# Scores of sparse query blocks: the low part of the queries times the high part of the keys in 64-row tiles, two heads at once, in a new order of all work

## The chip, the cores and the metric

The kernel runs on one core of one Trainium2 chip. The metric is the device time of one execution in microseconds, and three executions were timed: 767.21, 767.59 and 769.55 us, median 767.59 us. One more execution was profiled.

## What is computed

Block-sparse attention over 4 batches of 8 heads, followed by a gated two-layer network (cut; softmax and the last product are written short):

```python
scores = scale * np.matmul(q, k.transpose(0, 1, 3, 2))      # q, k, v: 4 x 8 x 768 x 64
mask = np.abs(blk_i - blk_j) <= window                       # window 1, blocks of 32 rows
mask = mask | (blk_i == 0) | (blk_j == 0) | (blk_i == n_blocks - 1) | (blk_j == n_blocks - 1)
for qb in range(n_blocks):
    for kb in sampled_blocks[qb]:                            # 3 sampled blocks
        mask[qb * block:(qb + 1) * block, kb * block:(kb + 1) * block] = True
scores = np.where(mask, scores, -1000000000.0)
attn = softmax(scores)                                       # over the last axis
x = (attn @ v), heads side by side: 3072 x 512
g = x @ w_gate                                               # 512 x 1536
silu = g * (1.0 / (1.0 + np.exp(-g)))
return (silu * (x @ w_val) @ w_out)                          # 1536 x 512
```

A query block of 32 rows attends to eight key blocks: the first, the last, three around its own and three sampled ones. The first and last query block of each batch attend to everything.

## The kernel before

**Chunks.** The 24 query blocks of a batch are put four to a tile of 128 rows. Batch 0 is worked in three chunks of two tiles (chunks 0 to 2), batches 1 to 3 in two chunks of three tiles each (chunks 3 to 8). For every chunk the kernel does attention and then the network: `ffn_in` (24 products of 12 matmuls each, line 1749; for chunks 0 and 1 in f32, line 1743) and `ffn_out` (per tile of 128 rows 36 matmuls, line 1812).

**Split numbers.** Batch 0 is worked in f32. In batches 1 to 3 every f32 number is held as two f16 numbers, a high and a low part. Keys are split in `load_kv` (ACT line 410 for the high part, DVE line 413 for the low one, two of each per 256 tokens) and turned by a DMA transpose (line 764, issued from SP) so that of each head the 64 partitions 0 to 63 hold the high part and the partitions 64 to 127 the low part. The queries of a tile lie twice, on partitions 0 to 63 and again on 64 to 127, as a high tile and a low tile.

**One sparse query block** (`block`, line 1116). The keys of its eight key blocks are copied to a ring (`keys`, lines 1133 to 1136, DVE), its values come by DMA. `scores` (line 1157) then runs for each half `g` of the heads (even or odd) and each of the two query parts `l` four matmuls, one for every `u`: head `2u+g`, 128 rows by 32 columns at column position `32u`, 256 keys. All 128 partitions are contracted, so that a query part meets both key parts at once. Four such matmuls lie beside each other in the array and run together; a block has 4 such steps of four matmuls. The scores of a block fill one PSUM bank (256 for even heads, 256 for odd heads). DVE adds the mask and takes the maximum (`top`, line 1171), ACT takes the exponential (lines 1186 and 1189) and splits it (410), DVE makes the low part (413), a DMA transposes it (1212), and TensorE multiplies by the values (`product`, line 1224, also 128x32 tiles). Two blocks are a pair: their scores are one task of 32 matmuls, named `qk`, their products share a bank, which DVE sums and scales (1240, 1243) and TensorE transposes (`x_turn`, line 1249). There are 33 pairs in batches 1 to 3.

**Batch 0** (`pair0`) makes its scores with f32 matmuls of 64 rows by 32 columns (line 1388), two heads in the two halves of the rows, each half with its own PSUM bank. `full_rows` and `full_rows0` work the two query blocks that attend to everything.

**The order** of all work is a list written out by hand, `TURN` (2750 tasks). Each engine takes its own tasks in that order and waits at the head of its queue for what the task needs. Buffers are rings: `qk` has two PSUM banks, `pv` two, `ffn` four. The numbers given to `add` as costs are not used by this order.

Of the kernel before, what the change touches and what calls it, by code (L numbers as in the profile page):

```python
# [9 lines left out]
F16 = mybir.dt.float16  # L10
# [242 lines left out]
def tile_block_sparse_attn_swiglu(  # L253
# [865 lines left out]
    def block(ci, b, bt, o, sub, n, qb, col, rank, tsc, pv, both):  # L1119
# [24 lines left out]
        def gathered():  # L1144
            nc.gpsimd.indirect_dma_start(  # L1145
                vf[0:96, 1, :], None, bt.vd, bass.IndirectOffsetOnAxis(ap=vidx[0:96, qb : qb + 1], axis=0)
            )

        qk, e, pp, pts = Buf("qk"), Buf("e"), Buf("pp"), Buf("pts")
        c = {}  # L1150

        def scores():
# [758 lines left out]
```

## Time and profile before

| | |
|---|---|
| median of 3 executions | 767.59 us |
| span of the profiled execution, first to last instruction | 765.5 us |
| what lies around the span, against the median | 2.1 us |
| TensorE (PE) busy | 736.9 us, 96% |
| VectorE (DVE) busy | 567.3 us, 74% |
| ScalarE (ACT) busy | 479.7 us, 63% |
| GpSimd (POOL) busy | 240.0 us, 31% |
| scores of sparse blocks, line 1157: 1056 matmuls | 35.0 us |

An engine is busy while one of its instructions runs. A matmul's record begins when its first column enters the array and lasts until its last result is out, so the records of matmuls that follow each other overlap: what a matmul takes of TensorE is read from the distance of the starts, not from its duration. The chain of waits goes back from the last instruction, at each step to what released it. "Idle before" is time in which the engine stood still just ahead of an instruction, with the instruction that ended the wait.

### The profile page before, as it was taken

The page shows a single profiled execution, that of the slowest core. Times are in us where ns is not written, and L with a number is a line of the kernel's source. Part 1 is how long each engine was busy: PE and PEld are TensorE (multiplying, and loading weights), DVE is VectorE, ACT ScalarE, POOL GpSimd, SP SyncE. Part 2 cuts the span into 40 slices and gives each one's busy share as a digit, 9 for nine tenths or more (in the row PEclk, how much of TensorE's full clock was granted, in tenths as well). Part 3 has the DMA queues.
Part 4 walks back from the last instruction along what each step waited for, and adds up shares of the span by engine and source line. Part 5 has one row for each costly group of instructions (what it writes and reads, how often), then busy time and mean ns, then how long its engine had stood idle before and what let it go on. Part 6 is the DMA issues. An engine that isn't in the chain of part 4 may idle for free.

```text
span 765.5 us, 22137 instructions
## 1 busy us (share of the span) xinstructions
PE 736.9 (96%) x8793; PEld 467.1 (61%) x8793; DVE 567.3 (74%) x1581; ACT 479.7 (63%) x1117; POOL 240.0 (31%) x290
## 2 busy tenths in 40 slices
PE   4899999999999999999999999999999999999998
PEld 3576788774686566545665566545665566555655
DVE  6999999987999998456898878647986677633220
ACT  4999655876887776745796665755764664443211
POOL 4887022222044422211343331302243333202210
PEclk9899999999999999999999999999999999999999
DMA  8856577376499996968779988787766854450001
GB/s 284 252 180 211 186 256 257 102 230 158 95 216 202 199 182 111 208 210 201 172 173 177 226 209 196 137 189 165 157 159 116 192 127 102 82 88 15 1 1 42
DMA packets 156472, 123.75 MB, mean 162 GB/s; under 512 B 113456, under 2 KB 124080, under 8 KB 156368
## 3 DMA queue, kind: packets, MB, share of 16 engines
q1 hardware_dynamic: 150736, 105.03, 57.5%
q0 software_dynamic: 5632, 17.31, 9.3%
q8 instruction: 69, 1.13, 0.6%
q14 instruction: 35, 0.29, 0.1%
HBM read 84.55 MB, written 11.01 MB: 125 GB/s over the span
## 4 chain that ended last, share of the span: by engine, by line
PE 64%; DVE 19%; ACT 5%; DMA 4%; issue 4%; POOL 1%; SPq 1%; DVEq 0%; POOLq 0%; ACTq 0%
PE p L1749 31%; PE po L1812 22%; PE qk L1157 3%; PE pv L1224 2%; DMA ptsf<-ppf 2%; DVE pp L413 1%; DVE act L1758 1%; DVE act L1763 1%; DVE w2all L451 1%; DVE w2all L452 1%; DVE kring L1135 1%; DVE e L1171 1%; PE pv L1249 1%; PE pvf L1011 1%; PE qkf L940 1%
## 5 line engine op out<-in xcount | busy, mean ns | idle before, releaser
L1749 PE MATMUL p<-xall,w1t 128*128 128x384 f16 (+1 forms) x2016 | 323.7, 319 | 1.0 <-DVE act L1758 1.0
L1749 PEld LDWEIGHTS <-w1t 128*128 128x128 f16 x2016 | 193.8, 98 | 117.0 <-issue 5.9
L1771 POOL TENSOR_TENSOR h<-act,h 128x384 f16<-128x384 f32 (+1 forms) x108 | 102.4, 952 | 333.9 <-ACT h L1768 330.4
L1812 PE MATMUL po<-w2all,h 128*128 128x512 f16 (+1 forms) x900 | 192.5, 371 | 0.3 <-DVE act L1758 0.3
L1812 PEld LDWEIGHTS <-h 128*128 128x128 f16 x900 | 86.4, 98 | 93.9 <-issue 1.6
L1145 POOL DMA_INDIRECT w2all<-vd,vidx x66 | 65.0, 985 | 92.6 <-PE pv L1224 83.1
L1743 PE MATMUL p<-xall,w1t 128*128 128x256 f32 x384 | 87.8, 383 | 3.6 <-DVE act L1758 2.5
L1758 DVE SCALAR_TENSOR_TENSOR act<-act,p 128x384 f32<-128x384 f32 (+1 forms) x108 | 54.3, 504 | 47.1 <-ACT act L1754 46.7
L1768 ACT CAST h<-act 128x384 f16<-128x384 f32 (+1 forms) x108 | 50.4, 471 | 61.8 <-DVE act L1763 61.6
L1743 PEld LDWEIGHTS p<-xall,w1t 128*128 128x128 f32 x384 | 71.0, 190 | 15.9 <-DVE act L1758 3.6
L1754 ACT ACTIVATE act<-p,gsc 128x384 f32<-128x384 f32 (+1 forms) x84 | 46.8, 558 | 52.4 <-PE p L1749 31.9
L1189 ACT ACTIVATE e<-e,nb,es 128x256 f32<-128x256 f32 x132 | 78.2, 593 | 2.2
L413 DVE SCALAR_TENSOR_TENSOR pp<-e,pp 128x512 f16<-128x512 f32 x66 | 51.0, 778 | 15.4 <-ACT pp L410 14.2
L1763 DVE SCALAR_TENSOR_TENSOR act<-act,hs,p 128x384 f32<-128x384 f32 (+1 forms) x84 | 49.4, 591 | 11.4 <-PE p L1749 9.1
L1171 DVE CUSTOM_DVE_ANT_1 e<-qk,msk 128x256 f32<-128x256 f32 x132 | 49.3, 418 | 2.5 <-PE qk L1157 2.2
L1687 POOL TENSOR_TENSOR sqx<-sqx 128x768 bf16<-128x768 bf16 (+3 forms) x18 | 22.3, 1238 | 61.0 <-ACT sqx L1683 60.4
L410 ACT ACTIVATE pp<-e 128x512 f16<-128x512 f32 x66 | 40.6, 624 | 0.6
L1135 DVE COPY kring<-kst 128x256 f16 x198 | 38.4, 253 | 3.0 <-PE qk L1157 1.5
L1644 ACT ACTIVATE ot<-po,oc 128x512 f32<-128x512 f32 (+1 forms) x25 | 16.6, 664 | 33.0 <-PE po L1812 27.3
L1519 ACT CAST xall<-pv 128x256 f16<-128x256 f32 x36 | 13.0, 364 | 36.3 <-PE pv L1249 36.3
L1157 PE MATMUL qk<-kring,qs 128*32 128x256 f16 x1056 | 35.0, 273 | 0.0
L1186 ACT ACTIVATE nb<-mx,es 128x2 f32<-128x2 f32 x66 | 19.1, 289 | 25.0 <-DVE mx L1171 24.3
(200 smaller groups left out, 991.5 us busy)
## 6 DMA issues: line engine op xcount, KB each, us to landing
stage<-in_w_dram SPq DMA_DIRECT2D x36, 512.0 KB, 6.6
w2all<-vd SPq DMA_DIRECT2D x66, 192.0 KB, 4.1
qraw<-in_q_dram SPq DMA_DIRECT2D x18, 512.0 KB, 4.5
out_dram<-ot SPq DMA_DIRECT2D x19, 256.0 KB, 2.8
qn<-in_q_dram SPq DMA_DIRECT2D x36, 128.0 KB, 4.1
stage<-in_v_dram SPq DMA_DIRECT2D x9, 512.0 KB, 5.5
vd<-stage SPq DMA_DIRECT2D x9, 512.0 KB, 2.8
stage<-in_k_dram SPq DMA_DIRECT2D x9, 512.0 KB, 6.2
```

The costliest lines, as they stand in the source:

```text
L413: nc.vector.scalar_tensor_tensor(lo, src, scale, hi, op0=ALU.mult, op1=ALU.subtract)
L1145: nc.gpsimd.indirect_dma_start(vf[0:96, 1, :], None, bt.vd, bass.IndirectOffsetOnAxis(ap=vidx[0:96, qb : qb + 1], axis=0))
L1157: nc.tensor.matmul(stv[u * BLK : (u + 1) * BLK, g].rearrange("p s k -> p (s k)"), o.q[:, l, u, g, col : col + BLK], kg[:, 2 * u + g].rearr ...
L1171: nc.vector.tensor_tensor_reduce(ev[:, g], stv[:, g], o.g.msk[:, qb, :].unsqueeze(2).broadcast_to([P, 8, BLK]), scale=1.0, scalar=-3.0e38, ...
L1189: nc.scalar.activation(ev[:, g], ev[:, g], AF.Exp, bias=nb_[:, g : g + 1], scale=o.g.es[:, 0:1], accum_out=both["rs"][:, n % 2, g : g + 1],)
L1743: nc.tensor.matmul(t[:, 0:tc_], w[:, i + 1, k_ * P : (k_ + 1) * P], x_k(k_), start=k_ == 0, stop=k_ == NKT - 1)
L1749: nc.tensor.matmul(t[:, 0:tc_], w_[:, f, m, k_, :], x_k(k_, l), start=i == 0, stop=i == 11)
L1758: nc.vector.scalar_tensor_tensor(a_, a_, 1.0, pg.tile[:, 0:tc_], op0=ALU.add, op1=ALU.mult)
L1763: nc.vector.scalar_tensor_tensor(a_, a_, sc, pw.tile[:, 0:tc_], op0=ALU.mult, op1=ALU.mult)
L1768: nc.scalar.copy(hv(f)[:, 0, :], act.tile[:, 0:tc_])
L1771: nc.gpsimd.tensor_tensor(hv(f)[:, 1, :], act.tile[:, 0:tc_], hv(f)[:, 0, :], op=ALU.subtract)
L1812: nc.tensor.matmul(po.tile[:, cs], hv(f)[:, l, ts_], w2h[:, f, m, cs], start=f == 0 and i == 0, stop=f == NF - 1 and i == 2)
```

## The change

In batches 1 to 3 the high query part is multiplied with all 128 partitions as before (8 matmuls of 128x32 a block, two steps of four). The low query part is multiplied with the high key part alone, 64 partitions, in tiles of 64 rows by 32 columns: an even head in rows 0 to 63, an odd head in rows 64 to 127, so that eight matmuls lie in the array beside each other. The product of the low query part and the low key part falls away. For this the keys of odd heads are stored with the halves swapped (high part on partitions 64 to 127). The two halves of the heads write to two different PSUM banks; the two blocks of a pair share these two banks, each taking 256 columns of each. In `load_kv` a high or low instruction for keys now takes the even or the odd heads of both 128-token halves, and the two DMA transposes of 256 tokens are issued after both low parts. The number of instructions is unchanged everywhere. `TURN` is a new list of the same 2750 tasks; on TensorE 312 of 573 tasks stand at another place, none further than 11 places. The diff without the list:

```diff
@@ -729,10 +729,12 @@
 
         def views(i, tt):
 
-            dst = parts[i].tile.bitcast(F16)
-            pat = "p (t h l d) -> p t h l d" if what == "k" else "p (t l h d) -> p t h l d"
-            dst = dst.rearrange(pat, h=H, l=2, d=D)
-            return dst[:, tt, :, 0, :], dst[:, tt, :, 1, :], raws[i][1]().rearrange("p t (h d) -> p t h d", d=D)[:, tt]
+            dst, src = parts[i].tile.bitcast(F16), raws[i][1]()
+            if what == "k":
+                four = dst.rearrange("p (u g x d) -> p u g x d", g=2, x=2, d=D)[:, :, tt]
+                return four[:, :, tt, :], four[:, :, 1 - tt, :], src.rearrange("p t (u g d) -> p (t u) g d", g=2, d=D)[:, :, tt]
+            dst = dst.rearrange("p (t l h d) -> p t h l d", h=H, l=2, d=D)
+            return dst[:, tt, :, 0, :], dst[:, tt, :, 1, :], src.rearrange("p t (h d) -> p t h d", d=D)[:, tt]
 
         done = []
         for i in range(3):
@@ -755,7 +757,8 @@
                 h_ = add("ACT", 0.63, high, [t] + los, rank, take=pi if first else [], use=ru + ([] if first else pi))
                 l_ = add("DVE", 0.68, low, [h_], rank, use=ru + pi)
                 los.append(l_)
-                if what == "k":
+            if what == "k":
+                for tt in range(2):
 
                     def turn(i=i, tt=tt):
                         if i == 0 and tt == 0:
@@ -767,7 +770,7 @@
                         )
 
                     f0 = i == 0 and tt == 0
-                    done.append(add("SP", 1.3, turn, [l_], rank, behind=None if f0 else done[0], take=[bt.ks] if f0 else [],
+                    done.append(add("SP", 1.3, turn, los, rank, behind=None if f0 else done[0], take=[bt.ks] if f0 else [],
                                     use=pi + ([] if f0 else [bt.ks]), dma=1.7))
             if what == "v":
 
@@ -1105,13 +1108,12 @@
                 if not b:
                     pair0(ci, o, sub, n, sparse[n], qbs.index(sparse[n]) * BLK, r)
                     continue
-                pv, both = Buf("pv"), {}
+                pv, both = Buf("pv"), {"qk": [Buf("qk"), Buf("qk")]}
                 two = [block(ci, b, bt, o, sub, n + i, sparse[n + i], qbs.index(sparse[n + i]) * BLK, r + 0.05 * i, tsc, pv, both)
                        for i in range(2)]
                 first = [next(x) for x in two]
-                qks = [x[2] for x in first]
-                a = in_turn("qk", "PE", 1.0, lambda first=first: [x[1]() for x in first], [x[0] for x in first] + [o.done], r,
-                            take=qks, use=[o.qs])
+                a = in_turn("qk", "PE", 0.67, lambda first=first: [x[1]() for x in first], [x[0] for x in first] + [o.done], r,
+                            take=both["qk"], use=[o.qs])
                 for x in two:
                     for _ in x:
                         pass
@@ -1146,31 +1148,45 @@
                 vf[0:96, 1, :], None, bt.vd, bass.IndirectOffsetOnAxis(ap=vidx[0:96, qb : qb + 1], axis=0)
             )
 
-        qk, e, pp, pts = Buf("qk"), Buf("e"), Buf("pp"), Buf("pts")
+        qk, e, pp, pts = both["qk"], Buf("e"), Buf("pp"), Buf("pts")
         c = {}
 
+        def score_of(g):
+            if n % 2 == 0 and qk[g].tile is None:
+                get(qk[g], f"qk_{nq}_{g}")
+            return qk[g].tile[:, n % 2 * 256 : (n % 2 + 1) * 256]
+
         def scores():
-            stv = get(qk, f"qk_{nq}").rearrange("p (g s k) -> p g s k", g=2, k=BLK)
+            st = [score_of(g) for g in range(2)]
             for g in range(2):
-                for l in range(2):
-                    for u in range(4):
-                        nc.tensor.matmul(
-                            stv[u * BLK : (u + 1) * BLK, g].rearrange("p s k -> p (s k)"),
-                            o.q[:, l, u, g, col : col + BLK],
-                            kg[:, 2 * u + g].rearrange("p s k -> p (s k)"),
-                            start=l == 0,
-                            stop=l == 1,
-                            tile_position=(0, u * BLK),
-                        )
+                for u in range(4):
+                    nc.tensor.matmul(
+                        st[g][u * BLK : (u + 1) * BLK],
+                        o.q[:, 0, u, g, col : col + BLK],
+                        kg[:, 2 * u + g].rearrange("p s k -> p (s k)"),
+                        start=True,
+                        stop=False,
+                        tile_position=(0, u * BLK),
+                    )
+            for u in range(4):
+                for g in range(2):
+                    half = slice(g * D, (g + 1) * D)
+                    nc.tensor.matmul(
+                        st[g][u * BLK : (u + 1) * BLK],
+                        o.q[half, 1, u, g, col : col + BLK],
+                        kg[half, 2 * u + g].rearrange("p s k -> p (s k)"),
+                        start=False,
+                        stop=True,
+                        tile_position=(g * D, u * BLK),
+                    )
 
         def top():
             ev = get(e, f"e_{nq}").rearrange("p (g s k) -> p g s k", g=2, k=BLK)
-            stv = qk.tile.rearrange("p (g s k) -> p g s k", g=2, k=BLK)
             mx = c["mx"] = small_t([P, 2], "mx", f"mx_{nq}")
             for g in range(2):
                 nc.vector.tensor_tensor_reduce(
                     ev[:, g],
-                    stv[:, g],
+                    score_of(g).rearrange("p (s k) -> p s k", k=BLK),
                     o.g.msk[:, qb, :].unsqueeze(2).broadcast_to([P, 8, BLK]),
                     scale=1.0,
                     scalar=-3.0e38,
@@ -1253,11 +1269,11 @@
         vl = add("SP", 1.4 if new else 0.5, values, bt.v_done + v_read[slot], rank + V_AT, dma=1.6 if new else 0.9, many=3 if new else 1)
         vi = add("POOL", 1.0, gathered, bt.v_done + [t_tab] + v_read[slot], rank + V_AT, dma=0.9)
         kc = add("DVE", 0.95 if new else 0.69, keys, bt.k_done + [o.loaded] + k_read[slot], rank, use=[bt.ks, o.regbuf])
-        yield kc, scores, qk
+        yield kc, scores
         a = stage_last["qk"]
         k_read[slot] = [a]
         plan.key = f"b{ci}.{sub}.{n}"
-        a = in_turn("top", "DVE", 0.7, top, [a, tsc, full_exp[0]], rank, take=[e], use=[qk, o.g.mb])
+        a = in_turn("top", "DVE", 0.7, top, [a, tsc, full_exp[0]], rank, take=[e], use=qk + [o.g.mb])
         a = in_turn("exp", "ACT", 1.45, power, [a], rank, use=[e])
         if n % 2:
             both["inv"] = add("DVE", 0.28, inv, [a], rank)
```

## Rows read from the trace of the kernel before

**Rows 1.** The page, parts 1, 2 and 4: busy time, granted clock, chain by engine.

```profile
PE 736.9 (96%) x8793; PEld 467.1 (61%) x8793; DVE 567.3 (74%) x1581; ACT 479.7 (63%) x1117; POOL 240.0 (31%) x290
...
PEclk9899999999999999999999999999999999999999
...
PE 64%; DVE 19%; ACT 5%; DMA 4%; issue 4%; POOL 1%; SPq 1%; DVEq 0%; POOLq 0%; ACTq 0%
```

**Rows 2.** Busy time by stretch of the span: PE, PEld, DVE, ACT, POOL, clock, DMA.

```profile
0.00:160.00 160.00, 141.46 (x1830) 111.01 (x1831) 145.97 (x328) 117.18 (x288) 71.63 (x122) 0.97 0.66 216
160.00:740.00 580.00, 573.21 (x6828) 342.70 (x6827) 421.37 (x1255) 360.21 (x827) 166.55 (x166) 1.00 0.70 153
```

**Rows 3.** Waits of PE from 160 us on: who, for whom, total us, times, longest.

```profile
PE pv L1249 <- DVE pts L1243: 3.5, 4, 1.6
PE pvf L1011 <- DMA ptsf<-ppf: 1.7, 2, 0.9
```

**Rows 4.** Groups of PE by shape: the scores; columns as in the page's part 5.

```profile
L1157 PE MATMUL qk<-kring,qs 128*32 128x256 f16 x1056 | 35.0, 273 | 0.0
```

**Rows 5.** Chain of waits, 360 to 400 and 578 to 624 us: start, us, what.

```profile
379.25 0.99 PE qk L1157 x32
380.24 0.34 PE pv L1224 x32
380.58 2.06 PE p L1749 x12
382.63 0.45 PE pv L1224 x32
383.09 0.87 PE qk L1157 x32
...
396.03 1.95 PE p L1749 x12
```

**Rows 6.** Timeline of PE at 584.3 us, products then scores: start, us, instruction.

```profile
584.12 0.22 PE L1224 MATMUL pv<-w2all,pts 128*32 128x128 f16 x1
584.17 0.39 PE L1157 MATMUL qk<-kring,qs 128*32 128x256 f16 x8
```

**Rows 7.** Timeline of PE at 193.6 us: last step of scores, then `ffn_out`.

```profile
193.37 0.28 PE L1157 MATMUL qk<-kring,qs 128*32 128x256 f16 x4
193.59 0.39 PE L1812 MATMUL po<-w2all,h 128*128 128x512 f16 x1
```

**Rows 8.** Timeline of PE at 46.2 and 61.7 us: batch 0, f32, shape changes.

```profile
45.99 0.22 PE L1448 MATMUL pv<-w2all,pts 128*32 128x64 f32 x1
46.14 0.40 PE L1388 MATMUL qk<-w1t 64*32 64x256 f32 x1
...
61.36 0.29 PE L1388 MATMUL qk<-kring,q 64*32 64x160 f32 x1
61.58 0.26 PE L1404 MATMUL qk<-dupm,ones_h 128*128 128x192 bf16 x1
```

**Rows 9.** Timeline of PE at 39.0, 39.5 and 39.7 us: scores of batch 0.

```profile
38.84 0.45 PE L1388 MATMUL qk<-w1t 64*32 64x256 f32 x8
...
39.09 0.63 PE L1388 MATMUL qk<-w1t 64*32 64x256 f32 x14
...
39.30 0.63 PE L1388 MATMUL qk<-w1t 64*32 64x256 f32 x13
```

**Rows 10.** Groups of DVE: the mask and maximum, the low parts of keys and values.

```profile
L1171 DVE CUSTOM_DVE_ANT_1 e<-qk,msk 128x256 f32<-128x256 f32 x132 | 49.3, 418 | 2.5 <-PE qk L1157 2.2 <-issue 0.2
L413 DVE SCALAR_TENSOR_TENSOR stage<-stage,ks 128x512 f16<-128x512 f32 x18 | 14.4, 813 | 3.8 <-ACT stage L410 3.7
L413 DVE SCALAR_TENSOR_TENSOR stage<-stage,vs 128x512 f16<-128x512 f32 x18 | 13.7, 768 | 1.3 <-ACT stage L410 1.2
```

**Rows 11.** Timeline of SP's queue, 505 to 530 us: key transposes of batch 3.

```profile
510.15 10.55 SPq L764 DMA_TRANSPOSE kst<-stage  x5
```

284 rows, old and new, of the table TURN are left out of this document.

## The prediction

> **What bounds the kernel now.** First the page: TensorE is busy for 96% of the span, DVE for 74%, and the chain that ended last runs over TensorE for 64% [rows 1]. Then the busy times by stretch: up to 160 us, where the weights are decoded, DVE is the fullest engine (146.0 of 160) and TensorE has gaps. From 160 to 740 us TensorE is busy for 573.2 of 580 us while DVE has 421.4 and ACT 360.2 [rows 2]. All scores that the change touches lie in this second stretch. Then the waits: what TensorE waits for there is nearly all two things, the scaling of a pair ahead of its transposition (3.5 us in four waits, the longest 1.6) and the transposed probabilities of the full rows (1.7 us) [rows 3]. Its granted clock is full in every slice but the first [rows 1], 1.00 in the second stretch [rows 2], the higher of its two levels, 2.4 GHz. So from 160 us on the kernel is as long as TensorE's work in its order, and a microsecond of TensorE added or taken away there is one of the span, apart from the 6.8 us in which it stands still.
>
> **What a step of scores costs.** The 32 matmuls of a pair take 0.87 us in the chain where they follow products of the same tile shape [rows 5]. They are eight steps of four beside each other, so a step takes 0.87/8 = 0.109 us; 256 columns at 2.4 GHz are 0.107 us. The scores are thus bound by columns, not by instructions: 1056 of them fill 35.0 us with a mean record of 273 ns [rows 4], but only 33 x 0.87 = 28.7 us of starts.
>
> **What the change removes.** A block needs three steps instead of four: two for the high query part, one of eight matmuls for the low part. Do eight tiles of 64x32 run at once? Batch 0 shows it: eight records in flight within 0.45 us, each about 0.40 long, and the following eights start 0.21 us after each other (39.09, 39.30) [rows 9]. An f32 record takes two passes, 2 x 256/2.4 GHz = 0.213 us, so eight 64-row tiles cost what one costs. 66 blocks x 1 step x 0.109 us = 7.2 us less.
>
> **What the change adds on TensorE.** The array must go from 128x32 tiles to 64x32 and back, and the rows price that. Where products (128x32) are followed by scores (128x32), the starts are 0.05 us apart [rows 6], which is the 128 columns of the product (0.053 us): nothing is lost. Where the scores are followed by 128x128 tiles, the last four start at 193.37 to 193.38 us and the next at 193.59 [rows 7]: 0.21 us, of which 0.107 are columns, so 0.10 us is lost. From 128x32 to 64x32, the very change in question: 45.99 to 46.14 = 0.15 us, less 64 columns in two passes (0.053 us), again 0.10 us; from 64x32 back: 61.36 to 61.58 = 0.22 us less 160 columns in two passes (0.133 us), 0.09 us [rows 8]. The chain says the same in longer pieces: scores after another shape 0.99 us instead of 0.87, twelve matmuls of line 1749 after narrow tiles 2.06 instead of 1.95, a block's products 0.45 instead of 0.34 [rows 5]. The exact 0.15 - 0.053 = 0.097 us is the value I take; the ends are 0.09 and 0.12.
>
> How many more are there? In a pair the order is: high part of the first block, its low part, high part of the second, its low part. That is three changes inside the task, 33 x 3 = 99. A fourth comes where 128x32 products follow the scores at once, which before was free: written out from the new list, 13 of the 33 tasks. The other moves on TensorE bring narrow and wide tasks into contact 6 times more. Together 118 changes; the old list has 161 places where neighbouring matmuls differ in shape, the new one 279. 118 x 0.097 = 11.4 us more (10.6 to 14.2 at the ends). Further, a step of eight has four more starts than one of four. Four scores start within 0.01 us [rows 7], eight in batch 0 within 0.05 [rows 9]; at the first rate it is 0.013 us, 66 x 0.013 = 0.9 us, at the second 0.04 and 2.6 us. I take 0.9, the row of the same number type.
>
> The sum on TensorE: -7.2 + 11.4 + 0.9 = +5.1 us; with the low ends +4.3, with the high ones +9.6. As much of it is taken up by waits as TensorE stands still, 6.8 of 580 us [rows 2], some 0.1 us.
>
> The Trainium skill ("TensorEngine Tiling (Array Packing)", "Key Properties") says that a change of the tiling mode, not only of the tile, drains TensorE; rows 6 to 8 agree, with 0.10 us. The same page ("Theoretical Speedup") gives a factor of up to 2 for a contraction of at most 64; that alone would leave the 7.2 us as a gain, which is the first rival below.
>
> **Off TensorE.** The maximum over a block reads half of two banks instead of one bank, in the same two instructions of 418 ns [rows 10]: no cost in time. But both banks now come free only after both blocks' maxima, so the first is held some two maxima longer, 2 x 0.42 = 0.8 us. Only the next task that takes a `qk` bank can feel it; the chain has the nearest two tasks of scores 3.8 us apart (379.25 and 383.09) [rows 5], so nothing is paid here; without that distance it would be up to 0.8 us a pair. The split of keys has the same counts; its longer stride costs between nothing and the 45 ns by which the low part of keys (813) already exceeds that of values (768) [rows 10], at most 0.8 us of DVE over 18 instructions, beside a TensorE that has work. The first key transpose of each 256 tokens waits for a further high and low part, some 1.5 us, but the last one of a batch not: five of them already spread over 10.55 us [rows 11]. Behind them on SP's queue stand value loads and stores. Between nothing and 1.3 us (one more transpose of about that length to issue after the last split) for each of three batches; I take nothing, since TensorE has products of the network to do there.
>
> **The new order.** Apart from the 6 changes counted above I find no side to it: on DVE's queue the last split of the weights stands behind the same tasks but for one, and between a block's scores and its products the new list has at least 11 us of TensorE work, the old one 12.8. What an order can win is bounded by what stands still: 6.8 us from 160 to 740, and in the first 160 us the 14.0 us of DVE [rows 2], of which about half is its start. I put the effect at 0, +-4 us.
>
> **Forecast.** The profiled execution would go from 765.5 to 770.5 us; with the 2.1 us by which the median lies above that span, 767.6 + 5 = 772.6 us, 0.65% slower. (Measurements of this kernel can tell some 0.3%, 2.3 us, from no change.)
>
> **Rivals.**
> 1. The shape changes inside a task cost nothing, because f16 tiles that keep their 32 columns need not empty the array. Then 7.2 us are won and 0.9 lost: 761.3 us, faster. It decides as soon as a change costs less than 6.3/118 = 0.053 us. For it: the change of shape from 128x32 to 64x32 is shown in f32 only. Against it: that change and all others show the same 0.09 to 0.10 us, in both number types [rows 7, 8]. Chance 0.13.
> 2. The new order pays back 3 to 8 us, by fewer waits of TensorE and an earlier end of the decoding. 764.5 to 769.6 us, centre 767. For it: 6.8 and 14.0 us stand still [rows 2]. Against: positions hardly differ. Chance 0.17.
> 3. The new order costs more waits. In it 10 transpositions of pairs stand at most 3 us of TensorE work behind their products, before it was 6, and this wait is the largest of TensorE (3.5 us, up to 1.6 each) [rows 3]. Four more at 1 to 1.6 us: +4 to +6, 776.6 to 778.6 us. Chance 0.13.
> 4. The change doesn't do what it says: the two row halves run one after the other. Then no step is saved, 772.6 + 7.2 = 779.8 us. Batch 0 speaks against it [rows 9]. Chance 0.04.
>
> **How the numbers follow.** The forecast has 0.53 and spans 769.5 to 776. Faster than 765.3: rival 1 (0.13) and the better end of rival 2 (0.05), 0.18. Within 0.3%, 765.3 to 769.9: the rest of rival 2 (0.12) and the lower edge of the forecast (0.04), 0.16. Slower: 0.66. The range leaves out rival 1 and rival 4, 0.17, and runs from the better end of rival 2 to the worse of rival 3: 764.5 to 778.6.
>
> **What would show it.** In the profile after, eight low-part matmuls of 64x32 start within about 0.03 us and the next 128x32 matmul 0.20 us after the last of them; a pair takes about 0.90 us between its first and last start (two times 0.35 and 0.20 between) instead of 0.87 - 0.11 = 0.76, and there are about 279 changes of shape. TensorE's busy share from 160 us on stays as high. The forecast is wrong if those starts are 0.11 us apart (rival 1), if the waits of [rows 3] shrink or grow by more than 2 us (rivals 2, 3), or if only four of the eight start together (rival 4).

## The result and the profile after

The changed kernel takes 773.72 us (median of 7 executions, 771.04 to 777.83) against 768.5 us of the kernel before in the same comparison (median of 7, 767.21 to 772.77). The ratio is 1.008, 95% interval 1.0055 to 1.0104: slower, by some 5 to 6 us, where 772.6 us and +5.0 were forecast. In a second comparison, with 12 executions of the changed kernel and 29 of the one before (run e6 below), it is 1.0044 (1.0015 to 1.0073), some 3.4 us. The ratios, here and below, leave out executions that took over 1.5% longer than the fastest of their kernel (three of e7's twelve and one of e9's six), while the medians beside them are of all.

The page of the changed kernel, the line of [rows 1] and the two groups that the scores have now (columns as there and as in [rows 4]):

```profile
PE 742.4 (96%) x8793; PEld 456.5 (59%) x8793; DVE 565.4 (73%) x1581; ACT 481.9 (62%) x1117; POOL 240.9 (31%) x290
...
PE 77%; DVE 10%; DMA 8%; issue 2%; ACT 2%; SPq 0%; POOL 0%; DVEq 0%; ACTq 0%
...
L1163 PE MATMUL qk<-kring,qs 128*32 128x256 f16 x528 | 26.5, 276 | 0.0
L1174 PE MATMUL qk<-kring,qs 64*32 64x256 f16 x528 | 20.0, 280 | 0.0
```

The number of matmuls is the same. TensorE is busy 5.5 us longer (742.4 against 736.9), and the chain that ended last runs over it for 77% instead of 64%. The profiled execution has a span of 774.5 us, 9.0 longer than that of before, but it is one of the longer ones (776.7 us against the median of 773.7). From 160 to 740 us TensorE is as full as before (answering [rows 2]):

```profile
160.00:740.00 580.00, 573.53 (x6787) 329.19 (x6786) 421.12 (x1260) 360.18 (x824) 162.71 (x165) 1.00 0.71 154
```

Up to 160 us TensorE was busy 3.8 us less than before (137.7 against 141.5), DVE 4.7 less (141.3 against 146.0). Nothing of the change lies there but the order, and the order is not shown to be the reason: in the profiled execution of e6, the same kernel, TensorE has 139.3 there and DVE 147.9. So the busy times of whole executions differ by more than what is looked for. The scores are compared better from their first matmul to TensorE's last: the kernel before, the changed kernel, and the changed kernel in e6 (columns as in [rows 2], the fourth row a part of the second):

```profile
192.60:762.20 569.60, 563.08 (x6814) 338.74 (x6813) 394.83 (x1192) 338.81 (x789) 159.07 (x159) 1.00 0.68 145
193.88:771.18 577.30, 571.57 (x6823) 329.61 (x6822) 394.28 (x1187) 339.95 (x789) 156.57 (x159) 1.00 0.67 144
190.39:766.51 576.12, 569.88 (x6823) 329.12 (x6822) 394.28 (x1187) 340.17 (x789) 156.50 (x159) 1.00 0.69 145
297.30:300.70 3.40, 3.40 (x13) 1.77 (x11) 3.30 (x10) 1.26 (x3) 0.00 (x0) 0.50 0.28 74
```

In the profiled execution of the changed kernel the granted clock was 0.50 from 297.3 to 300.7 us, the lower of the two levels (1.2 GHz); TensorE had stood still for 2.5 us shortly before, up to 296.5 us. Twelve matmuls of line 1765 take 3.72 us there and 2.12 us in e6. That is 1.7 us of extra work that is not of the scores (half of 3.4), and neither the page's digits nor the clock of the long stretches, 1.00, show it. Without it the two executions of the changed kernel agree: 569.9 and 569.9 us. Of these, 1.9 us are 9 matmuls of `ffn_out` (9 x 512 columns at 2.4 GHz) that the new order puts behind the first scores and the old one ahead of them (6823 against 6814 matmuls). So the scores' stretch has 569.9 - 1.9 - 563.1 = 4.9 us more work, where 5.1 were forecast. TensorE stands still in it for 6.5 us before and 6.2 in e6: the extra work is paid one for one.

A pair of blocks in the changed kernel, in the timeline of TensorE (start, us, instruction), answers [rows 5 to 8]:

```profile
459.22 0.39 PE L1163 MATMUL qk<-kring,qs 128*32 128x256 f16 x8
459.54 0.30 PE L1174 MATMUL qk<-kring,qs 64*32 64x256 f16 x8
459.77 0.40 PE L1163 MATMUL qk<-kring,qs 128*32 128x256 f16 x8
460.11 0.30 PE L1174 MATMUL qk<-kring,qs 64*32 64x256 f16 x8
460.34 0.52 PE L1240 MATMUL pv<-w2all,pts 128*32 128x128 f16 x32
```

The eight low-part matmuls do run together: the row of eight is 0.30 us long while one record lasts 0.28, so they start within 0.02 us (the profile models the ends of matmuls, but both lengths have the same end). One step of theirs stands for two steps of four. But from the first start of the high part to that of the low part it takes 0.32 us, of which two steps are 0.22: 0.10 us is lost. From the low part back to the next high part it takes 0.23 us, of which one step is 0.107 and the spread of eight starts 0.02: again 0.10. The first start of the pair to the first of the products that follow is 460.34 - 459.22 = 1.12 us; eight steps without a change of shape are 0.87 [rows 5]. Over all 33 pairs the distance from the first to the last start is 0.91 us in the median, where the prediction had 0.90. The trace has 279 places where neighbouring matmuls differ in shape, the number that was counted from the list.

### The profile page after: what moved, and what is told of

The parts are those of the page before. It is cut to its first block, busy times and chain, and to the rows that moved or that the text cites. A ratio compares the mean times of both kernels' runs of the same rounds, so it can differ in the third digit from the quotient of the medians.

```text
span 774.5 us, 22161 instructions
## 1 busy us (share of the span) xinstructions
PE 742.4 (96%) x8793; PEld 456.5 (59%) x8793; DVE 565.4 (73%) x1581; ACT 481.9 (62%) x1117; POOL 240.9 (31%) x290
## 4 chain that ended last, share of the span: by engine, by line
PE 77%; DVE 10%; DMA 8%; issue 2%; ACT 2%; SPq 0%; POOL 0%; DVEq 0%; ACTq 0%
PE p L1765 38%; PE po L1828 22%; DMA pts<-pp 4%; PE p L1759 4%; PE pv L1240 3%; PE qk L1163 2%; PE qk L1174 2%; DMA w2all<-in_v_dram 2%; DVE w1t L452 2%; DVE w1t L451 1%; DVE w1t L450 1%; PE qkf L943 1%; PE pvf L1014 1%; DMA qn<-in_q_dram 1%; PE pv L1265 1%
## 5 line engine op out<-in xcount | busy, mean ns | idle before, releaser
L1187 DVE CUSTOM_DVE_ANT_1 e<-qk,msk 128x256 f32<-128x256 f32 x132 | 49.6, 418 | 17.1 <-PE qk L1174 16.9
L413 DVE SCALAR_TENSOR_TENSOR pp<-e,pp 128x512 f16<-128x512 f32 x66 | 47.6, 727 | 9.5 <-ACT pp L410 8.8
L1256 DVE TENSOR_REDUCE pts<-pv 128x256 f32<-128x512 f32 x33 | 22.7, 687 | 24.8 <-PE pv L1240 24.8
L1137 DVE COPY kring<-kst 128x256 f16 x198 | 36.6, 240 | 0.2 <-issue 0.2
L1240 PE MATMUL pv<-w2all,pts 128*32 128x64 f16 (+1 forms) x2112 | 31.9, 207 | 4.3 <-DMA pts<-pp 4.2
L1240 PEld LDWEIGHTS <-pts 128*32 128x32 f16 x2112 | 24.7, 97 | 17.8 <-issue 10.8
```

Of the source, the lines that this page charges most:

```text
L413: nc.vector.scalar_tensor_tensor(lo, src, scale, hi, op0=ALU.mult, op1=ALU.subtract)
L1187: nc.vector.tensor_tensor_reduce(ev[:, g], score_of(g).rearrange("p (s k) -> p s k", k=BLK), o.g.msk[:, qb, :].unsqueeze(2).broadcast_to([ ...
L1240: nc.tensor.matmul(to[rows_, g, 0:w_], pq[:, g, l, cc, u], vg[:, cc, 0:w_, 2 * u + g, :], start=i == 0, stop=i == 3, tile_position=(0, u * ...
```

## The experiments

Each kernel ran beside the kernel before on the same chip, in two groups of four kernels with 29 executions of the kernel before in each: median 778.69 us in the first group (e1, e2, e3, e5), 769.4 us in the second. The chips differ by 1.2%, so ratios are compared.

**The changed kernel in the order of the kernel before.** The edit is the list alone; in the changed kernel seven key transposes and one norm need something later, and stand there.

```diff
-TURN = [  the new list
+TURN = [  the list of the kernel before, renumbered
```

> The changed kernel with the order of the kernel before (seven key transposes and one norm of batch 3 with its followers stand a little later, since they need or take something that comes free later). If the changes of tile shape are the cause: 109 more of them than in the kernel before, 109 x 0.097 = 10.6 us, less 7.2 us of steps, plus 0.9 us of starts: +4.3 us on the kernel before, about 772.8 us. If the new order is the cause: the time of the kernel before, about 768.5 us. If both: between.

Measured: 783.26 us, ratio 1.006 (1.0041 to 1.0078), +4.7 us where +4.3 was expected. The loss is there without the new order.

**The kernel before in the new order.**

```diff
-TURN = [  the list of the kernel before
+TURN = [  the new list, renumbered
```

> The kernel before with the new order alone, scores as before. If the changes of tile shape inside the scores are the cause: only the 6 changes that the order itself adds, +0.6 us, about 769 us. If the new order is the cause: about 773.7 us. The transpositions of pairs that now stand closer to their products would show as longer waits of TensorE on the scaling.

Measured: 778.3 us, ratio 0.9995 (0.9973 to 1.0017). The order by itself costs nothing that can be measured. The transpositions that it puts closer to their products are not punished either: the wait of TensorE on the scaling is 1.1 us there, against 3.5 in [rows 3] (two of the three longest waits of TensorE from 160 us on, columns as in [rows 3]).

```profile
PE pv L1226 <- DMA pts<-pp: 4.7, 3, 1.8
...
PE pv L1251 <- DVE pts L1245: 1.1, 2, 0.8
```

What it has instead is a wait of the products on the transposed probabilities (4.7 us in three waits), which [rows 3] does not have.

**The changed kernel without row tiles.**

```diff
             for g in range(2):
-                for u in range(4):
-                    nc.tensor.matmul(
...
-                        tile_position=(g * D, u * BLK),
-                    )
+                for l in range(2):
+                    for u in range(4):
+                        nc.tensor.matmul(
+                            st[g][u * BLK : (u + 1) * BLK],
+                            o.q[:, l, u, g, col : col + BLK],
+                            kg[:, 2 * u + g].rearrange("p s k -> p (s k)"),
+                            start=l == 0,
+                            stop=l == 1,
+                            tile_position=(0, u * BLK),
+                        )
```

> The changed kernel without its 64-row tiles: the low query part meets all 128 partitions again, four steps a block, all 128x32. The new order, the two shared banks and the swapped keys stay. If the row tiles are the cause: 5.1 us less than the changed kernel apart from the order's own part, about 769 us, the time of e2. If the shared banks or the order of the key transposes are the cause: about 773.7 us or, with the four steps back, more. The difference to e2 is the price of the shared banks and the swapped keys; I expect 0 within 1.5 us.

Measured: 778.69 us, ratio 0.9989 (0.9964 to 1.0015). With the shared banks, the swapped keys, the later key transposes and the new order all in place, the loss is gone. What is left of the change as its cause is the 64-row step, and the difference to e2 (0.9995) prices everything else at nothing within the intervals, which together are 2.6 us either way.

**The parts of a pair sorted.** The same 32 matmuls; the high part of both blocks first, then the low part of both. The first matmul of a bank opens it, the last closes it.

```diff
-lambda first=first: [x[1]() for x in first]
+lambda first=first: [first[i][1](m, 2 * m + i) for m in range(2) for i in range(2)]
...
-        def scores():
+        def scores(part, place):
...
+            begin, end = place == 0, place == 3
...
```

> The changed kernel with the scores of a pair sorted by part: the high part of both blocks, then the low part of both. The same 32 matmuls and the same columns, one change of tile shape inside the task instead of three. If shape changes are the cause: 66 fewer, 66 x 0.10 = 6.4 to 6.6 us less than the changed kernel, about 767 us, and 213 changes in the trace. If the number of 64-row matmuls, the two banks or the order are the cause: unchanged, about 773.7 us.

Measured: 776.95 us, ratio 0.9991 (0.9973 to 1.0009), with 213 changes of shape in the trace. In the same group e1 has 270 and 1.006, so 57 fewer are worth 0.69% of 778.7 us, 5.4 us or 0.094 us each (3.3 to 7.4 us by the two intervals together, 0.06 to 0.13 each), in two different orders that e2 found equal. The timeline of a pair, columns as above:

```profile
457.22 0.61 PE L1165 MATMUL qk<-kring,qs 128*32 128x256 f16 x16
457.76 0.41 PE L1177 MATMUL qk<-kring,qs 64*32 64x256 f16 x16
458.10 0.42 PE L1243 MATMUL pv<-w2all,pts 128*32 128x128 f16 x19
```

The pair takes 458.10 - 457.22 = 0.88 us to the start of the products that follow, instead of 1.12. The 0.54 us from the first row to the second are four steps (0.44) and one change; sixteen low-part matmuls with no change between them take 0.34 us to the next shape, two steps and one change.

**The changed kernel again**, in the second group:

> The changed kernel itself, beside the others of this group on the same chip. All theories: its ratio to the kernel before, 1.008 as in the result, within 0.3%.

Measured: 773.43 us, ratio 1.0044 (1.0015 to 1.0073), 0.36% lower than in the result, so a little outside the 0.3% that was expected; the interval of the result begins at 1.0055. Its profiled execution has a span of 769.8 us.

**Sorted, and the low part first where that saves a change at the end.** In 6 tasks the products follow but don't precede; these end with the high part.

```diff
+LOW_FIRST = {1216, 1351, 1875, 2617, 1242, 1022}
...
-lambda first=first: [x[1]() for x in first]
+lambda first=first, no=no: [first[i][1](m ^ (no[0] in LOW_FIRST), 2 * m + i) for m in range(2) for i in range(2)]
```

> As e3 (the parts of a pair sorted, one change of tile shape inside a task), and in the 6 tasks that are followed but not preceded by 128x32 products the low part goes first, so that the task ends in the shape that follows. New order. If the changes of tile shape set the time: 33 inside, 7 at ends and 6 of the order against the kernel before, 46 x 0.097 = 4.5 us, less 7.2, plus 0.9: -1.8 us, 0.998 of the kernel before, 0.6 us less than e3. If e3 only gained by something else than the changes, no difference to the changed kernel or a loss.

Measured: 768.73 us, ratio 0.9986 (0.9955 to 1.0018), 207 changes. Against the changed kernel of the same group this is -0.58%, 4.5 us for 72 changes, where 7.0 were expected by the price of 0.097; the two intervals together allow 1.2 to 7.8 us. In the profiled executions of the two, TensorE is busy 8.6 us less from the first score on (561.3 against 569.9), so what fell short there is not the price of the changes. It is the lowest of the complete kernels, but not to be told from the kernel before.

**The same in the order of the kernel before.**

```diff
+LOW_FIRST = {1604, 1351, 2288, 1267, 1875, 1047, 2617, 1242}
```

> The same with the order of the kernel before (as in e1), the low part first in 8 tasks. 33 changes inside and 2 at ends: 35 x 0.097 = 3.4 us, less 7.2, plus 0.9: -2.9 us, 0.996 of the kernel before, if the changes set the time. If sorting brings nothing: 1.006 as e1.

Measured: 769.38 us, ratio 1.0001 (0.9973 to 1.0029), 196 changes, where 0.996 was expected. The loss of e1 (1.006) is gone, but the gain of 2.9 us is not there. TensorE's busy time from the first score to its last matmul (as in the result) and its longest waits show where it stayed in the profiled execution:

```profile
196.82:767.69 570.87, 560.90 (x6814) 329.16 (x6813) 393.77 (x1192) 338.93 (x789) 159.72 (x159) 1.00 0.68 146
...
PE pv L1248 <- DMA pts<-pp: 3.7, 3, 2.0
PE pv L1273 <- DVE pts L1267: 3.5, 4, 1.7
```

TensorE is busy 2.2 us less than before in this stretch (560.9 against 563.1), near the 2.9 expected, but it stands still for 10.0 us, 6.5 before. The scaling (3.5) and the full rows (1.3) are waited for as in [rows 3]; the wait on the transposed probabilities (3.7) is new. This is one execution, and one of the longer ones (773.2 us); that such waits took the gain in all of them is likely and not shown.

**Without the low query part.**

```diff
-                        stop=False,
+                        stop=True,
...
-            for u in range(4):
-                for g in range(2):
-                    half = slice(g * D, (g + 1) * D)
-                    nc.tensor.matmul(
...
-                        tile_position=(g * D, u * BLK),
-                    )
```

> The changed kernel without the low query part: its matmuls are left out, so the scores lack that product. It prices the whole of the 64-row steps: 66 steps of about 0.107 + 0.023 us, 8.6 us, and 112 changes of tile shape at 0.10 us, 11.2 us, so 19.8 us less than the changed kernel, 0.982 of the kernel before, if the changes are paid in full. If the changes of shape are hidden and only the steps count: 8.6 us less, 0.997. If TensorE does not set the time in that stretch: less than 4 us.

Measured: 760.08 us, ratio 0.985 (0.9812 to 0.9887). Against the changed kernel in the same group this is -1.9%, 14.9 us for 66 steps of 64-row tiles and their changes. That is more than the steps alone (8.6) and less than the full price (19.8): three quarters of the price come through (11.3 to 18.6 us by the two intervals). The columns of 66 steps are 7.1 us, so most of what the 64-row steps cost is not their columns. The profile, of the longest of the six executions (765.9 us), shows where the rest can go. From the first score to the last matmul (compare e6 in the result):

```profile
195.72:760.34 564.62, 555.25 (x6295) 328.22 (x6294) 393.68 (x1187) 339.20 (x789) 157.66 (x159) 0.99 0.66 147
```

In three short stretches of it (from 225.6, 246.0 and 297.2 us, 10.2 us together) the granted clock was 0.50 to 0.51, which makes the work about 5.1 us longer; without that it is 550.2 us, 19.7 less than in e6 (569.9), the full price. Waits took back some more: TensorE stands still for 9.4 us, 6.2 in e6. The other five executions had a mean granted clock of 0.991, against 0.9935 over the twelve of e6, so by an estimate 0.0025 x 760 = 1.9 us of their missing 5 went to the clock; that waits took the other 3 in them too is not shown.

The kernels in one table, by steps a block and changes of shape in the trace:

| kernel | steps | changes | ratio to before | interval |
|---|---|---|---|---|
| before | 4 | 161 | 1 | |
| e2, before in the new order | 4 | 167 | 0.9995 | 0.9973 to 1.0017 |
| e5, no row tiles | 4 | 167 | 0.9989 | 0.9964 to 1.0015 |
| the change | 3 | 279 | 1.008 and 1.0044 | 1.0055 to 1.0104 and 1.0015 to 1.0073 |
| e1, the change in the old order | 3 | 270 | 1.006 | 1.0041 to 1.0078 |
| e3, parts sorted | 3 | 213 | 0.9991 | 0.9973 to 1.0009 |
| e7, sorted, low part first in 6 | 3 | 207 | 0.9986 | 0.9955 to 1.0018 |
| e8, the same in the old order | 3 | 196 | 1.0001 | 0.9973 to 1.0029 |
| e9, no low part | 2 | 167 | 0.985 | 0.9812 to 0.9887 |

## Why the prediction was right

**The bound.** Right. From 160 to 740 us TensorE is busy for 573.2 us before and 573.5 after, and 4.9 us more work from the first score on stand beside 5 to 6 us of more time in the first comparison and 3.4 in the second. That the whole execution's busy time grew by 5.5 us is partly chance: in it are the 1.7 us at the lower clock and the varying stretch up to 160 us, and in e6 the busy time is 739.6 us, 2.7 more than before. The clock was misread in a detail: the page has it lower in the second slice, not the first, and a 9 there stands for 0.9 or more, not for full.

**The steps saved.** Right. Eight 64x32 tiles run together in f16 as in f32: sixteen of them in e3 take the two steps and one change that they should.

**The price of a change of shape.** Right, and it was the step that decided. The rows priced it at 0.09 to 0.10 us in shapes of batch 0 and in f16 between others; in the changed kernel the very change, 128x32 to 64x32 and back in f16, costs 0.10 us each way (medians 0.095 and 0.103). Rival 1 (no cost, 761.3 us) fell with the five rows of the pair above, and e3 shows from the other side that taking 66 of the changes away takes the loss away. The Trainium skill ("TensorEngine Tiling (Array Packing)", "Key Properties") has the drain as a rule; the trace adds its size.

**The count of changes.** Right, 279. It had to be taken from the new list, since 19 of the 118 lie between tasks and not in the scores.

**The spread of eight starts.** Eight low-part matmuls start within 0.02 us where four start within 0.01, so 0.013 more per step as taken, not the 0.04 that f32 allowed.

**The order.** Put at 0, and e2 has 0.9995. Rival 2 and rival 3 both fell. Rival 3's mechanism, transpositions closer to their products, was wrong in itself: in e2 the wait on the scaling became shorter. The distance in TensorE work was a poor measure of it; of the waits in the trace of before the two longest (1.6 and 1.3 us) had 2.9 and 4.0 us of work ahead of them, and places with 1.9 to 2.1 waited 0.04 us at most. In the changed kernel the wait on the scaling shrank by 2.1 us, and that on the full rows is gone, which by the prediction's own sign would count against it; but a wait of similar size came up elsewhere, on the transposed probabilities (against [rows 3]):

```profile
PE pv L1240 <- DMA pts<-pp: 4.2, 3, 2.5
PE pv L1265 <- DVE pts L1259: 1.4, 2, 1.2
```

That the sum stayed the same (6.5 and 5.7 us from the first score on) is luck: nothing in the prediction says that one wait takes the place of another.

**Off TensorE.** The cost of the banks, the keys and the transposes was put at nothing, and e5 against e2 bears it out. DVE now waits longer for the scores before the maxima, 16.9 us in all where [rows 10] has 2.2, which the prediction did not see coming (below the changed kernel, in the last row the kernel before in the new order, e2).

```profile
L1187 DVE CUSTOM_DVE_ANT_1 e<-qk,msk 128x256 f32<-128x256 f32 x132 | 49.6, 418 | 17.1 <-PE qk L1174 16.9
L413 DVE SCALAR_TENSOR_TENSOR stage<-stage,vs 128x512 f16<-128x512 f32 x18 | 14.6, 813 | 1.8 <-ACT stage L410 1.6
L413 DVE SCALAR_TENSOR_TENSOR stage<-stage,ks 128x512 f16<-128x512 f32 x18 | 13.6, 769 | 3.8 <-ACT stage L410 3.5
L1173 DVE CUSTOM_DVE_ANT_1 e<-qk,msk 128x256 f32<-128x256 f32 x132 | 49.8, 418 | 12.6 <-PE qk L1159 10.7 <-PE pvf L1013 0.6 <-DVE mx L1173 0.5
```

Most of it is the order's and not the banks': e2, with the banks of before, has 10.7 us of it, e5, with shared banks and no row tiles, 13.4, and e8, with shared banks in the old order, 3.3. It costs nothing, since e2 and e5 are no slower. DVE has room in this stretch (421 of 580 us busy).

**The stride of the keys.** The low part of keys takes 769 ns now and that of values 813, the other way round than in [rows 10]. The layout is not the cause: the kernels in the old order, e1 and e8 with the new layout among them, all have 813 to 815 for keys and 768 for values, those in the new order, e2 with the old layout among them, 769 to 771 and 813 to 814. It goes with the order; that what runs beside them is the reason is likely and not shown. In the trace of before single ones of the 18 for keys take up to 1195 ns, and the median is 751:

```profile
L413 DVE SCALAR_TENSOR_TENSOR stage<-stage,ks x18: 734/751/1195, 176.7 to 512.7; 128x512 f16<-128x512 f32 x18
```

(Least, median and largest duration.)

**Open.** Why the two comparisons of the same two kernels give 1.008 and 1.0044, with intervals that only just meet: the granted clock of the changed kernel's executions, 0.992 on average in the first and 0.9935 in the second, accounts for about 1 us of the difference by an estimate (0.0014 x 770), but those of the kernel before in the first are not on record. What makes the waits on the transposed probabilities come and go with the kernel. And what stretches single pairs of scores on the chip of the first group: in e1 the 33 pairs take 33.9 us in all between first and last start, 30.4 in e6, at nearly the same median (0.92 and 0.91).

## What to carry to other kernels

Packing two small products into the two halves of the array saves columns, but each passage between tile shapes costs TensorE about 0.10 us here, as much as a step of 256 columns; a saved step pays only if it brings fewer than one change of shape with it. So sort by shape before counting the saving: the same matmuls cost 1.12 us a pair when the shapes alternated and 0.88 when they were sorted. And where an engine is full, count such passages in its instruction list, between tasks too: the trace of the old kernel already held their price, at places that had nothing to do with the change.

## What the runs showed of the hardware

Changes of tile shape cost nearly the same in every pair of shapes that these traces hold often: 128x32, 64x32 and 128x128, in f16, bf16 and f32, with medians of 92 to 105 ns from start to start less the columns of the last matmul, at the full clock; the few with 128x64 and 64x64 agree. Not expected was that the mean time of one and the same DVE instruction shape moves by 45 ns with the order of the other work alone (e1 and e2). And a short stretch at the lower clock, which no digit of the page shows, cost 1.7 us in one profile, a third of the effect that was looked for: before two single profiles are compared, look at how long the same matmuls take in both.
